# Query loads of the first two units in two-position packets, with two reorderings, in a retention kernel followed by a multiplicative FFN

## The chip, the cores and the metric

The kernel runs on one core of one Trainium2 chip. The metric is device time in microseconds of one execution, and lower is better. The time before is the median of three timed runs.

## What is computed

The reference computes retention attention with a decay per head, reshapes its output to one row per token, and feeds it to a feed-forward block whose two branches are multiplied.

```python
batch, n_heads, seq, head_dim = (8, 8, 576, 64)
n_tokens, d_model, d_ff = (4608, 512, 1024)

scores = scale * np.matmul(q, k.transpose(0, 1, 3, 2))
Dmat = np.where(rel >= 0, gamma[:, None, None] ** rel[None, :, :], 0.0)
attn = np.matmul(scores * Dmat[None, :, :, :], v)

x = attn.transpose(0, 2, 1, 3).reshape(B * S, H * D)
a = x @ w1
b = x @ w2
out = (a * b @ w3) @ w_out
```

Everything is float32. The weights reach the kernel as pairs of 32-bit words, eight bytes a value, and are turned into float32 on the chip.

## The kernel before, in words

**Units.** Two batch elements are treated together. The 576 positions are cut into five chunks, the first of 64 positions and four of 128. A pair of batch elements and a chunk make a unit `g`; there are 20 units, and unit 0 is the short chunk of the first pair.

**Attention of one unit.** `load` brings k, q and v of a unit into tiles `ld_k`, `ld_q`, `ld_v`, with a position on each partition and 64 floats of a head, 256 bytes, as one run. `scale` multiplies q and v by the decay of each position and head (`gq`, `gk`). `front` turns k and q with TensorE transposes into PSUM tiles `tp`, which ScalarE copies to `kT` and `qT`. `score` multiplies them (`sc`) and VectorE applies the causal mask (`pm`). `state` accumulates k times v over the chunks (`st`, copied by ScalarE to `sb`). `pv_state` and `pv` write the unit's output into `xps`, and ScalarE copies it to `xT`, the token matrix. Later units load q, and partly k, in blocks of 32 by 32 (`load_blocks`, tiles `bl_q`, `bl_k`) and turn them on VectorE (`front_blocks`); `scale_blocks` scales such q on GpSimd.

**Dense work.** `up` is one block of seven Strassen products of tokens with w1 and w2 (`up` tiles in PSUM, sums on VectorE in `plus`), and `down` is the same for the last product. While a dense block runs, `plus` takes one piece of other work from the list `aside` after each sum. In the first block, `up(..., first=True)`, one piece is taken before the first sum as well.

**Weights.** `conversion` turns each raw block (`raw`) into float32 in several steps on ScalarE and VectorE; `convert` runs a number of steps. The first dense block needs the four blocks "A" and the sums of `strassen_weights`.

**Order.** The order on each engine is the order of the program text, written out by hand. An instruction that waits holds back all that stand behind it on its engine. SyncE issues nearly all loads in that same order, and ScalarE issues that of the decays and of the first q. `keep_busy(n)` puts n matmuls of a 128 by 128 identity on TensorE; nothing reads their result.

The start of the program up to the first dense block is a straight list of calls. The part around the change reads, before:

```python
    load(1, "kq")
    ...
    scale(0, "q", engine=nc.vector)
    front(0, "k")
    keep_busy(4)
    front(0, "q")
    convert(2)
    score(0)
    scale(0, "v")
    state(0)
```

The decay of q arrives as `dq`, a head on each partition, and five TensorE transposes into `gps` with two VectorE copies give `gq`, a position on each partition.

Of the kernel before, what the change touches and what calls it, by code (L numbers as in the profile page):

```python
# [8 lines left out]
F32 = mybir.dt.float32  # L9
# [4 lines left out]
ALU = mybir.AluOpType  # L14
# [5 lines left out]
def kernel(  # L20
# [20 lines left out]
    P = 128  # L41
# [20 lines left out]
    const = ctx.enter_context(tc.tile_pool(name="const", bufs=1))  # L62
    wp = ctx.enter_context(tc.tile_pool(name="wp", bufs=1))
    ffn = ctx.enter_context(tc.tile_pool(name="ffn", bufs=2))
# [6 lines left out]
    pools = {}  # L71
# [13 lines left out]
    live = {}  # L85

    def load(g, names, engine=nc.sync):
        i, c = divmod(g, NC)
        sz = sizes[c]
        src = {"k": k, "q": q, "v": v}  # L90
        for nm in names:
            t = pools["ld"].tile([P, 2 * H, D], F32, tag="ld_" + nm, name="ld_" + nm)
            engine.dma_start(  # L93
                t[:sz], src[nm][2 * i:2 * i + 2, :, starts[c]:starts[c] + sz, :].rearrange("b h p d -> p (b h) d"))
            live[nm, g] = t

    dq = ffn.tile([P, 4, 2, TB], F32, tag="c", name="dq", bufs=1).rearrange("p a b s -> p (a b s)")[:H, :S]
    nc.scalar.dma_start(dq, decay_q)
    load(0, "k")
    load(0, "q", nc.scalar)  # L100

    ident = const.tile([P, P], F32, tag="ident", name="ident")
    make_identity(nc, ident)
# [16 lines left out]
    gps = acc.tile([P, NC, H], F32, tag="acc", name="gps")  # L120
    for c in range(NC):
        nc.tensor.transpose(gps[:sizes[c], c, :], dq[:, starts[c]:starts[c] + sizes[c]], ident[:H, :H])
    for c in (0, slice(1, NC)):
        n = short if c == 0 else P
        nc.vector.tensor_copy(gq[:n, c, :], gps[:n, c, :])

    def keep_busy(n):

        t = acc.tile([P, P], F32, tag="acc", name="idle")
        for _ in range(n):  # L130
            nc.tensor.matmul(t, ident, ident, start=True, stop=True)
# [53 lines left out]
    def front_blocks(g, names="kq"):  # L185
        c = g % NC
        n = sizes[c] // BL
        for nm in names:
            dst = pools["fr"].tile([P, 2, NP, P], F32, tag=nm + "T", name=nm + "T", bufs=1 if nm == "k" else 2)
            nc.vector.transpose(  # L190
                dst[:, :, :, :sizes[c]].rearrange("p b m (n x) -> p (b m) n x", x=BL),
                live["bl_" + nm, g][:, :, :n, :])
            live[nm + "T", g] = dst

    def scale(g, nm, scalar=False, engine=nc.gpsimd):
        c = g % NC
        sz = sizes[c]
        t, gam = live[nm, g], {"q": gq, "v": gk}[nm]
        t = t[:sz].rearrange("p (b h) d -> p b h d", b=2)
        if scalar:  # L200
            for h in range(H) if scalar is True else scalar:
                nc.scalar.mul(t[:, :, h, :], t[:, :, h, :], gam[:sz, c, h:h + 1])
            return
        engine.tensor_tensor(
            out=t, in0=t, in1=gam[:sz, c].unsqueeze(1).unsqueeze(3).to_broadcast([sz, 2, H, D]), op=ALU.mult)

    def front(g, names="kq"):
        c = g % NC
        sz = sizes[c]
        for nm in names:  # L210
            src = live[nm, g]
            dst = pools["fr"].tile([P, 2, NP, P], F32, tag=nm + "T", name=nm + "T",
                                   bufs=1 if nm == "k" and g >= NC else 2)
            for b in range(2):
                tp = acc.tile([P, NP, P], F32, tag="acc", name="tp")
                for p in range(NP):
                    h = b * H + 2 * p
                    nc.tensor.transpose(tp[:, p, :sz],  # L218
                                        src[:sz, h:h + 2, :].rearrange("p a d -> p (a d)"),
                                        ident[:sz, :sz])  # L220
                nc.scalar.copy(dst[:, b, :, :sz], tp[:, :, :sz])
            live[nm + "T", g] = dst

    def score(g):
# [100 lines left out]
    def load_block():  # L325
        n = loaded[0]
        if n == len(blocks):
            return
        key, w = blocks[n]
        t = raw.tile([P, CV, 2], I32, tag="raw", name="raw", bufs=5)  # L330
        if key[0] in ("A", "w12"):
            if key[0] == "A":
                _, r, f = key
                t4 = t.rearrange("p (j c n) t -> p j c n t", j=2, c=2)
                parts = [(t4[:, j], w[:, f * P:(f + 1) * P]) for j, w in enumerate((moe_w1, moe_w2))]
            else:
                _, fp, _, r = key
                parts = [(t.rearrange("p (c n) t -> p c n t", c=2), w[:, fp * QC:(fp + 1) * QC])]
            for t2, src in parts:
                src = src[2 * r * P:2 * (r + 1) * P]  # L340
                if r == 0:
                    nc.sync.dma_start(t2, src.rearrange("(c p) n t -> p c n t", p=P))  # L342
                else:
                    for half in range(2):
                        nc.sync.dma_start(t2[heads[half]],
                                          src.rearrange("(c a d) n t -> a d c n t", a=2, d=D)[1 - half])
        elif key[0] == "wo":
            src = w.rearrange("(a i x) n t -> i a x n t", i=KF, x=BL)[key[1]]
            for a in range(QP):
                nc.sync.dma_start(t[a * BL:(a + 1) * BL], src[a])  # L350
        else:
            _, ft, h = key
            src = w[ft * P:(ft + 1) * P].rearrange("(j r) (a h f) t -> h a r j f t", r=BL, a=QP, h=DF // CV)
            for a in range(QP):
                nc.sync.dma_start(t[a * BL:(a + 1) * BL].rearrange("p (j f) t -> p j f t", j=P // BL), src[h, a])
        live["raw", n] = t
        loaded[0] += 1
# [105 lines left out]
    def convert(n):  # L463

        for _ in range(n):
            if go_on() is not None:
                return
# [97 lines left out]
    aside, owed, spread, beside, loads = [], [], [], [], []  # L565
    g = 0
# [148 lines left out]
    load_block()  # L715
    load(0, "v")
    load_block()
    load(1, "kq")
    load_block()
    load(1, "v")  # L720
    load_block()
    scale(0, "q", engine=nc.vector)
    front(0, "k")
    keep_busy(4)
    front(0, "q")
    convert(2)
    score(0)
    scale(0, "v")
    state(0)
    convert_up_to(1)  # L730
# [27 lines left out]
    next(weight_sums)  # L758
    list(token_sums)
    list(weight_sums)  # L760
    aside.append(lambda: scale(2, "q", True))
    scale(2, "v")
    up(0, 0, 0, conv=[0, 0, 2, 2, 2], tail=False, first=True)
    front(2)
    convert(1)
    score(2)
    state(2)
# [364 lines left out]
    g = NC  # L1132
# [9 lines left out]
    for g in first_pair:  # L1142
        n = (1, 1, 2, 2)[g - NC]
        if not in_blocks[g + 2]:
            load(g + 2, "k")
            load_blocks(g + 2, "q")
        scale(g + 1, "v")
        if not in_blocks[g + 1]:
            front(g + 1, "k")
            front_blocks(g + 1, "q")  # L1150
        half = (n + 1) // 2
        if in_blocks[g + 1]:
            scale_blocks(g + 1)
            work(n - 1)
            aside.extend(lambda nm=nm: front_blocks(g + 1, nm) for nm in "kq")
            work(1)
            while aside:
                aside.pop(0)()
            half = 0
        if in_blocks[g + 2] and g + 2 < 2 * NC:  # L1160
            load_blocks(g + 2, "q")
            load_blocks(g + 2, "k")
        work(half)
        pv(g)()
        load(g + 2, "v", nc.scalar if in_blocks[g + 2] else nc.sync)
        if in_blocks[g + 2] and (g + 2) % NC != NC - 1:
            load(g + 2, "k")
        state(g + 1)
        score(g + 1)
        if not in_blocks[g + 2]:  # L1170
            scale_blocks(g + 2)
        if g == NC + 1:
            list(strassen_tokens(1, 0))
            forms = [(lambda h=h, second=second: spread.extend(weight_forms(h, second)),)
                     for h in halves for second in (False, True)]
            ups = [(up, 1, 0, fp) for fp in range(NQ)]
            todo.extend([*ups[:2], forms[0], *ups[2:], forms[2], (flush,), forms[1], (down, (1, 0), (1, 1)),
                         (down, (2, 2), (3, 2)), (open_second,), (down, (3, 0), (3, 1))])
        if not in_blocks[g + 1]:
            work(n // 2)  # L1180

    g = 2 * NC - 1
# [9 lines left out]
    g = 2 * NC  # L1192
# [15 lines left out]
    for g in range(2 * NC, G):  # L1208
        n = dealt[g - 2 * NC]
# [42 lines left out]
    g = G  # L1252
# [44 lines left out]
```

## Time and profile before

| | |
|---|---|
| median of 3 timed runs | 837.97 us (836.92 to 840.8) |
| profiled execution, its own time | 944.19 us |
| span of the profile | 942.5 us |
| mean granted TensorE clock in the profile | 0.846 |
| TensorE matmul busy | 931.7 us, 99% |
| VectorE, ScalarE, GpSimd busy | 545.4, 289.7, 224.4 us |
| bytes moved by DMA | 126.96 MB |

The profiled execution is longer than the timed runs; its clock is on record, that of the timed runs is not. A profile line gives start and duration in microseconds, then engine, source line, operation, the tile written and the tiles read, shapes and the number of instructions merged; what stands in brackets is the engine's idle time before it and what ended that. A float32 matmul stands in the trace as two records, so four identity matmuls are eight records. SPq and ACTq are the issuing sides of SyncE and ScalarE. In the first 30 us the queue that SyncE feeds moves 15,321 packets and 5.42 MB.

### The profile page before, as it was taken

The numbers are of one execution on the slowest core, as the hardware profiler recorded it, in microseconds if no ns is written. First come the engines' busy times: TensorE is split into PE (matmuls) and PEld (weight loads), VectorE is DVE, ScalarE is ACT, GpSimd is POOL, SyncE is SP. The second block draws the span as 40 slices with busy tenths as digits, with TensorE's granted clock in tenths as the row PEclk, the third lists the DMA queues.
The fourth block names the chain that finished last, engine by engine and source line by source line (L and its number), as shares of the span: only waits on it lengthen the run. The fifth ranks groups of instructions, "written<-read, shape, count | busy, mean of one in ns | idle before, by whom it ended". The sixth has DMA issues, their size and how long they took to land.

```text
span 942.5 us, 15780 instructions
## 1 busy us (share of the span) xinstructions
PE 931.7 (99%) x6101; PEld 818.4 (87%) x6101; DVE 545.4 (58%) x957; ACT 289.7 (31%) x601; POOL 224.4 (24%) x249
## 2 busy tenths in 40 slices
PE   8999999999999999899999999999999999999998
PEld 7999999533888998689999789998789998799976
DVE  4888888970544467644557643657545555535542
ACT  4776454560111111044343023331033320033200
POOL 1100010002003172015536015463016250044500
PEclk7888888888888888888888888888888888888888
DMA  9992543426045475967675146868245352135311
GB/s 187 225 222 74 83 122 98 133 62 99 1 86 111 74 224 197 319 173 194 170 193 154 41 88 207 215 192 160 57 116 192 119 184 73 40 131 187 118 29 40
DMA packets 197868, 126.96 MB, mean 135 GB/s; under 512 B 157848, under 2 KB 179608, under 8 KB 197792
## 3 DMA queue, kind: packets, MB, share of 16 engines
q1 hardware_dynamic: 167520, 50.14, 26.4%
q0 software_dynamic: 11632, 62.79, 20.4%
q10 hardware_dynamic: 18640, 13.02, 5.0%
q8 instruction: 48, 0.79, 0.4%
q14 instruction: 28, 0.23, 0.1%
HBM read 103.62 MB, written 22.28 MB: 134 GB/s over the span
## 4 chain that ended last, share of the span: by engine, by line
PE 95%; DMA 3%; SPq 1%; ACT 0%; POOL 0%; issue 0%; DVE 0%; ACTq 0%
PE po L637 26%; PE up L524 18%; PE up L1039 18%; PE seed L1039 13%; PE ps L477 7%; PE xps L299 4%; PE sc L233 4%; PE xps L274 2%; PE st L255 2%; PE tp L218 1%; DMA ld_v<-in_v_dram 1%; DMA kept<-wA 1%; DMA ld_q<-in_q_dram 1%; DMA out_dram<-ot 1%; SPq L93 0%; SPq L342 0%
## 5 line engine op out<-in xcount | busy, mean ns | idle before, releaser
L637 PE MATMUL po<-w3o,ab 128*128 128x256 f32 x552 | 145.0, 426 | 2.8 <-ACT ot L669 2.2
L637 PEld LDWEIGHTS po<-w3o,ab 128*128 128x128 f32 x552 | 109.4, 200 | 32.5 <-ACT ot L669 2.7
L1044 POOL TENSOR_TENSOR cc<-cc 128x384 f32<-128x384 f32 x112 | 109.3, 1002 | 5.2 <-ACT cc L1062 3.7
L1051 DVE TENSOR_TENSOR cc<-seed,cc 128x384 f32<-128x384 f32 x88 | 49.0, 557 | 91.9 <-PE seed L1039 85.4
L941 POOL DMA_DIRECT2D ra<-kept x53 | 30.0, 566 | 243.5 <-PE seed L1039 181.1
L1039 PE MATMUL up<-xT,ra 128*128 128x192 f32 x384 | 83.7, 360 | 0.0
L529 DVE TENSOR_TENSOR c<-up,c 128x384 f32<-128x384 f32 x80 | 44.0, 551 | 64.9 <-PE up L524 64.4
L524 PE MATMUL up<-xT,wA 128*128 128x192 f32 x384 | 80.5, 360 | 0.0
L637 PE MATMUL po<-wB,forms 128*128 128x256 f32 x288 | 75.8, 425 | 0.0
L524 PEld LDWEIGHTS up<-xT,wA 128*128 128x128 f32 x384 | 72.0, 197 | 1.4 <-issue 0.6
L1051 DVE TENSOR_TENSOR cc<-up,cc 128x384 f32<-128x384 f32 x88 | 48.5, 551 | 42.5 <-PE up L1039 39.8
L1039 PEld LDWEIGHTS up<-xT,ra 128*128 128x128 f32 x384 | 72.0, 198 | 1.3 <-issue 0.4
L637 PEld LDWEIGHTS po<-wB,forms 128*128 128x128 f32 x288 | 57.8, 201 | 15.2
L236 DVE TENSOR_TENSOR pm<-sc,mask 128x512 f32<-128x512 f32 (+1 forms) x80 | 45.4, 627 | 41.2 <-PE sc L233 41.1
L477 PE MATMUL ps<-wo,w3T 128*128 128x512 f32 x128 | 64.4, 673 | 0.0
L1058 ACT COPY seed<-up 128x384 f32<-128x384 f32 x56 | 25.9, 463 | 121.1 <-PE up L1039 118.5
L1039 PE MATMUL up<-ra 128*128 128x192 f32 x288 | 62.5, 359 | 0.0
L477 PEld LDWEIGHTS ps<-wo,w3T 128*128 128x128 f32 x128 | 25.5, 199 | 38.1 <-issue 37.8
L1039 PE MATMUL seed<-e,ra 128*128 128x192 f32 x256 | 57.4, 361 | 0.0
L1039 PEld LDWEIGHTS up<-ra 128*128 128x128 f32 x288 | 54.6, 198 | 0.2
L524 PE MATMUL up<-T,wS 128*128 128x192 f32 x256 | 53.5, 359 | 0.0
L181 POOL TENSOR_TENSOR bl_q<-bl_q,gqs 128x512 f32<-128x512 f32 (+1 forms) x26 | 27.9, 1093 | 103.3 <-DMA bl_q<-in_q_dram 101.3
(126 smaller groups left out, 1550.9 us busy)
## 6 DMA issues: line engine op xcount, KB each, us to landing
ra<-kept POOLq DMA_DIRECT2D x53, 896.0 KB, 4.9
raw<-in_moe_w_dram SPq DMA_DIRECT2D x72, 128.0 KB, 3.1
out_dram<-ot ACTq DMA_DIRECT2D x54, 128.0 KB, 2.3
bl_q<-in_q_dram SPq DMA_DIRECT2D x192, 32.0 KB, 3.0
bl_k<-in_k_dram SPq DMA_DIRECT2D x136, 32.0 KB, 3.0
raw<-in_moe_w_dram SPq DMA_DIRECT2D x16, 256.0 KB, 6.3
ld_k<-in_k_dram SPq DMA_DIRECT2D x8, 512.0 KB, 5.9
raw<-in_moe_w_out_dram SPq DMA_DIRECT2D x32, 128.0 KB, 2.7
```

The source lines that it names most:

```text
L181: nc.gpsimd.tensor_tensor(out=part, in0=part, in1=gqs[:, :, n0:n0 + n].unsqueeze(3).to_broadcast([P, NP, n, BL]), op=ALU.mult)
L233: nc.tensor.matmul(sc[j][:sz, p, :sz], kT[hs, b, p, :sz], qT[hs, b, p, :sz], start=True, stop=True)
L236: nc.vector.tensor_mul(pm[:sz, b, j, :, :sz], sc[j][:sz, :, :sz], mask[:sz, :sz].unsqueeze(1).to_broadcast([sz, NP, sz]))
L299: nc.tensor.matmul(banks[r][heads[half], b, n, :sz], vs[:sz, b * H + 2 * p + j, :], pm[:sz, b, j, p, :sz], start=(c == 0 and m == 0), stop ...
L477: nc.tensor.matmul(ps, live["w3T", ft][:, g, :], live["wo"][:, g, :], start=(g == 0), stop=(g == KF - 1))
L524: nc.tensor.matmul(ps[:, w, :], a[:, w, r, :], b[:, r, :], start=(new and w == r == 0), stop=(w == r == 1), skip_group_check=True)
L529: nc.vector.tensor_add(c[:, to], ps, c[:, sb])
L637: nc.tensor.matmul(ps[nm], a[A][:, f, :], live["W"][B][:, f, :], start=(f == 0 and not on), stop=(f == NP - 1), skip_group_check=True)
L941: engine.dma_start(ring[n % 3], kept[n % 14 // 7][nm])
L1039: nc.tensor.matmul(ps[:, w, :], weight_of(slot, a, w), B[b], start=(new and w == 0), stop=True, skip_group_check=True)
L1044: nc.gpsimd.tensor_tensor(out=o, in0=o, in1=i, op=ALU.add)
L1051: nc.vector.tensor_add(c[:, j], ps, with_add[:, j])
```

## The change

It has three parts.

1. **q of units 0 and 1.** `load_pairs` replaces `load` for these two. A partition then holds two neighbouring positions of one batch element, so that one run is 512 bytes, and a unit takes two DMAs, one for each batch element. The decay in this arrangement is `gq2`, made by `decay_pairs`: for each of the two positions a VectorE copy of `dq` into `by`, a TensorE transpose into `gps` and a VectorE copy out. `scale` becomes two VectorE instructions of half the size, which write to another tile, `q2`. `front` copies each PSUM tile of q with two ScalarE instructions that write every second element. `decay_pairs(1)` and `keep_busy(7)` stand where `keep_busy(4)` stood.
2. **The third unit.** The transposes of unit 2 are put on `aside` and so run between the products of the first dense block instead of after it, with two empty entries ahead of them.
3. **Blocks.** In the loop over `first_pair`, where both q and k of the next unit come in blocks (units 7, 8 and 9), VectorE turns those of q first, then, after an empty entry, those of k.

```diff
+    def load_pairs(g, engine):
+        i, c = divmod(g, NC)
+        sz = sizes[c] // 2
+        t = live["q", g] = pools["ld"].tile([P, 2 * H, D], F32, tag="ld_q", name="ld_q")
+        for b in range(2):
+            engine.dma_start(
+                t[b * sz:(b + 1) * sz].rearrange("p (h j) d -> p h (j d)", j=2),
+                q[2 * i + b, :, starts[c]:starts[c] + 2 * sz, :].rearrange("h (i j) d -> i h (j d)", j=2))
...
-    load(0, "q", nc.scalar)
+    load_pairs(0, nc.scalar)
...
+    def decay_pairs(c):
+        n = sizes[c] // 2
+        for j in range(2):
+            by = ffn.tile([H, 2, n], F32, tag="T", name="by", bufs=5)
+            nc.vector.tensor_copy(by, dq[:, starts[c]:starts[c] + 2 * n].rearrange(
+                "h (i j) -> h j i", j=2)[:, j].unsqueeze(1).to_broadcast([H, 2, n]))
+            nc.tensor.transpose(gps[:2 * n, 2 * c + j, :], by.rearrange("h b i -> h (b i)"), ident[:H, :H])
+            nc.vector.tensor_copy(gq2[:2 * n, c, j], gps[:2 * n, 2 * c + j, :])
+
+    decay_pairs(0)
...
+        if nm == "q" and g < 2:
...
+            for j in range(2):
+                engine.tensor_tensor(out=to[:sz, j * H:(j + 1) * H], in0=t[:sz].rearrange("p (h j) d -> p j h d", j=2)[:, j],
+                                     in1=gq2[:sz, c, j].unsqueeze(2).to_broadcast([sz, H, D]), op=ALU.mult)
+            return
...
-                nc.scalar.copy(dst[:, b, :, :sz], tp[:, :, :sz])
+                if nm == "q" and g < 2:
+                    for c2 in range(2):
+                        nc.scalar.copy(dst[:, c2, :, :sz].rearrange("p m (i j) -> p m i j", j=2)[:, :, :, b],
+                                       tp[:, :, c2 * sz // 2:(c2 + 1) * sz // 2])
+                else:
+                    nc.scalar.copy(dst[:, b, :, :sz], tp[:, :, :sz])
...
-    load(1, "kq")
+    load(1, "k")
+    load_pairs(1, nc.sync)
...
     front(0, "k")
-    keep_busy(4)
+    decay_pairs(1)
+    keep_busy(7)
     front(0, "q")
...
-    aside.append(lambda: scale(2, "q", True))
+    aside.extend([lambda: scale(2, "q", True), lambda: None, lambda: None,
+                  lambda: front(2, "k"), lambda: front(2, "q")])
     scale(2, "v")
     up(0, 0, 0, conv=[0, 0, 2, 2, 2], tail=False, first=True)
-    front(2)
...
-            aside.extend(lambda nm=nm: front_blocks(g + 1, nm) for nm in "kq")
+            aside.extend([lambda: front_blocks(g + 1, "q"), lambda: None, lambda: front_blocks(g + 1, "k")])
```

More of the change, by code (lines that the diff above doesn't have):

```diff
@@ L125 @@
         nc.vector.tensor_copy(gq[:n, c, :], gps[:n, c, :])
+    gq2 = const.tile([P, 2, 2, H], F32, tag="gq2", name="gq2")
+    def decay_pairs(c):
[7 more added lines that the diff above has]
+    decay_pairs(0)
     def keep_busy(n):
@@ L198, in scale @@
         t, gam = live[nm, g], {"q": gq, "v": gk}[nm]
+        if nm == "q" and g < 2:
+            if not g:
+                live["q2"] = ffn.tile([P, 2 * KF, TB], F32, tag="ab", name="q2").rearrange("p f t -> p (f t)")
+            n = 2 * H * D
+            to = live["q", g] = live["q2"][:, g * n:(g + 1) * n].rearrange("p (h d) -> p h d", d=D)
+            for j in range(2):
+                engine.tensor_tensor(out=to[:sz, j * H:(j + 1) * H], in0=t[:sz].rearrange("p (h j) d -> p j h d", j=2)[:, j],
+                                     in1=gq2[:sz, c, j].unsqueeze(2).to_broadcast([sz, H, D]), op=ALU.mult)
+            return
         t = t[:sz].rearrange("p (b h) d -> p b h d", b=2)
@@ L217, in front @@
                     h = b * H + 2 * p
[L218 to L221, printed above, removed]
+                    x = src[:sz, h:h + 2, :].rearrange("p a d -> p (a d)")
+                    nc.tensor.transpose(tp[:, p, :sz], x, ident[:sz, :sz])
+                if nm == "q" and g < 2:
[4 more added lines that the diff above has]
+                    nc.scalar.copy(dst[:, b, :, :sz], tp[:, :, :sz])
             live[nm + "T", g] = dst
```

## The prediction

> **What bounds the kernel now.** I read the page's busy times first, then the list of what TensorE waited for.
>
> ```profile
> PE 931.7 (99%) x6101; PEld 818.4 (87%) x6101; DVE 545.4 (58%) x957; ACT 289.7 (31%) x601; POOL 224.4 (24%) x249
> ```
>
> TensorE has work in 99% of the span, so only what shortens its idle or slow stretches can show. 4.2 of its 10.8 idle us lie before 60 us, and the largest later wait, 2.2 us at 397 us, is on a ScalarE copy behind output stores, which the change doesn't touch. So I read the start: the chain of waits, then TensorE in order of time, then stretches of 3.4 us.
>
> ```profile
> 1.45 6.23 DMA ld_q<-in_q_dram
> ...
> 9.62 2.81 SPq L93
> ...
> 15.37 7.96 DMA ld_v<-in_v_dram
> 23.33 0.07 issue
> 23.39 1.91 POOL ld_v L204
> 25.31 0.04 issue
> 25.35 1.21 PE st L255 x32
> ```
>
> The last to arrive ahead of the dense block at 29.58 us is v of unit 1, and its load was issued late behind the others.
>
> ```profile
> 6.94 1.25 PE L131 MATMUL idle<-ident 128*128 128x128 f32 x8
> 9.05 0.90 PE L218 MATMUL tp<-ident,ld_q 64*128 64x64 f32 x8 [0.86 <-DVE ld_q L204]
> 9.97 1.97 PE L233 MATMUL sc<-qT,kT 64*64 64x64 f32 x32
> 12.59 1.98 PE L255 MATMUL st<-ld_v,ld_k 64*64 64x64 f32 x32 [0.64 <-POOL ld_v L204]
> ...
> 20.33 1.18 PE L218 MATMUL tp<-ident,ld_q 128*128 128x128 f32 x8 [0.61 <-PE idle L131]
> 21.66 2.26 PE L233 MATMUL sc<-qT,kT 64*128 64x128 f32 x32 [0.16 <-ACT qT L221]
> 23.86 1.21 PE L274 MATMUL xps<-qT,sb 64*64 64x128 f32 x32
> 25.35 1.21 PE L255 MATMUL st<-ld_v,ld_k 128*64 128x64 f32 x32 [0.28 <-POOL ld_v L204]
> ```
>
> That v makes TensorE wait only 0.28 us: a second chain, q of unit 0 to q of unit 1, is nearly as late.
>
> ```profile
> 5.80:9.20 3.40, 2.54 (x25) 2.14 (x24) 1.68 (x4) 0.65 (x2) 0.00 (x0) 0.85 1.23 212
> 9.20:12.60 3.40, 2.73 (x42) 2.36 (x41) 2.19 (x6) 2.87 (x5) 1.89 (x1) 0.50 1.19 207
> 12.60:16.00 3.40, 3.40 (x64) 3.40 (x64) 2.54 (x5) 1.36 (x3) 0.00 (x0) 0.50 1.36 222
> 16.00:19.40 3.40, 3.40 (x21) 3.28 (x18) 1.78 (x3) 2.85 (x6) 0.00 (x0) 0.50 1.18 272
> ```
>
> Third from the right is the granted clock: half from 9.2 to 19.4 us; then DMA share and GB/s. DMA is full throughout.
>
> **What the Trainium skill says.** "TensorE: Matmul & The Clock Gate", Part 1, says the clock halves after an idle window of about 3.4 us and returns after a busy one, and that windows run free of the kernel. The trace agrees: half clock lasts 10.2 us, three windows. The same page, Part 4, says transposes don't count as busy for the gate; here the window with 1.25 us of identity matmuls and short transposes lost the clock. "DMA: Bandwidth & Descriptors", Specifications, puts the smallest run at full rate at 512 bytes. The packet records of this trace have medians of 18 ns for 256 bytes, 27 for 512 and 46 for 1,024, so two 256-byte packets cost 36 and one of 512 costs 27.
>
> **Part 1, gain.** q of unit 0 is 1,024 packets of 256 bytes, 64 on each of 16 engines: 64 x 18 = 1.15 us become 32 x 27 = 0.86, 0.3 us less. Unit 1 is twice that, 0.6 us less. With v behind both, v of unit 1 can land about 0.9 us sooner (0 if packets are cut again, 1.6 if a packet's cost is the same at both sizes). Each unit issues one DMA more: on ScalarE's queue that is 0.74 us ahead of the decay `gk` and the table load (3.58 us to 4.3; the first copy is at 6.79, so it is hidden; `gk` still lands ahead of v, which it scales). On SyncE it is about 0.6 us ahead of a raw block and v of unit 1, and lies inside the time in which that queue is held back (the 2.81 us above).
>
> **Part 1, cost.** One pass of `decay_pairs` is copy, transpose, copy: 0.16 (row `gq<-gps`) + 0.05 (VectorE's end at 8.99 to TensorE's start at 9.04) + 0.24 (0.20 for such a transpose, and part of its weight load) + 0.04 + 0.16 = 0.65 us, and two follow each other: 1.3 us. In the changed program's order `decay_pairs(0)` stands after the two `gq` copies (end 6.66) and before k's transposes, so k's move from 6.29 to about 7.8; hidden, since q's scaling ends later. q's scaling starts at 7.96 in place of 7.77, two halves of 0.63, end 9.2. **The decisive step**: the transposes of `decay_pairs(1)` wait for VectorE copies that stand behind q's scaling, and `keep_busy(7)` and q's transposes stand behind them on TensorE. Until now the filler ran while q was awaited; now it starts when q is ready: 9.2 + 1.1 = 10.3. Seven matmuls are 14 records of 0.156 us at the granted 0.85 (1.25/8), 2.2 us, or of 0.22 at half clock (1.76/8), 3.1 us. So q's transposes start at 12.5 to 13.4, not at 9.05.
>
> The four ScalarE copies: a copy of 256 elements takes 0.37 us, one of 512 0.59, so 128 elements cost about 0.27; I assume no penalty for writing every second element (bounds 0 and twice). `score(0)` needs the third copy and starts at 13.6 to 14.8 (9.97 before). The delay doesn't pass on in full: `state(0)` had its own wait for v (12.59), and takes 1.2 at best, 2.0 at half clock, so it ends at 16.1 to 18.8, not 14.57. Behind it stand ScalarE's `sb` copy (0.58), three steps of the second raw block (2.25), two VectorE steps (1.4), then half of q's scaling of unit 1 (0.65; before it was 1.22 whole): 21.0 to 23.7. Transposes and three copies later `score(1)` starts at 22.8 to 25.9, against 21.66. Less the 0.28 that v no longer costs, the dense block starts 0.9 to 3.9 us later. The sooner landing of v is then off the path. The four extra transposes beyond this, and VectorE's 1.3 us for eight small copies, are in these sums.
>
> **Part 2.** The same 16 transposes and four copies move; nothing is added. `score(2)` waits 0.18 us for ScalarE's copy now; between products the copy is hidden. ScalarE's `c` copy comes about 2.3 us later and delays the product `ab` by 0.5 us on VectorE; `pm` follows at 44.3 and is needed at 48.08. Gain 0.2 us, bounds 0 to 0.5. Cover gone: nothing worse than now.
>
> **Part 3.** VectorE turns q at 296.4, 318.9 and 346.4, where it turned k. GpSimd ended their scaling at 290.8, 312.8 and 339.8. k of unit 8 is turned some 3 us later, done by 323.2, against `score` at 329.9; of unit 9 by 350.7, against 356.6. In these stretches TensorE has no wait. The sum pushed behind them (L613, 0.69 us) is read at about 366.9. On SyncE, blocks of q for units 8 and 9 can be issued 1.5 us sooner and those of k 1.5 us later, in the order in which the buffers are asked for. Zero; bounds -0.3 and +0.3.
>
> **Sum.** +0.9 to +3.9, less 0.2; I take +1.9, nearer the lower end because some windows may be granted full clock. Against the profile: 944.19 + 1.9. That execution is 12.7% above the median at a granted 0.846; the difference is in long products that the change leaves alone, and the start hangs on DMA, ScalarE and VectorE too, so I carry the same microseconds to 837.97: **839.9 us**.
>
> **Rivals.** *(a) Seven fillers win the clock back*: if the window holding them counts as busy, score, state and transposes run at 1.2 instead of 2.0 us. The delay is the lower end: 837.97 + 0.9 - 0.2 = 838.7. For: the fillers are what ended the half clock at 19.4. Against: they fill 2.3 of the 3.4 us to 12.6. *(b) Slower*: the half clock lasts longer, because the window in which unit 1's k and filler now fall is broken by the wait for its q. Eight transposes take 1.97 at half clock and 1.18 after, so each more window costs 3.4 x (1 - 1.18/1.97) = 1.4 us. With two, +1.9 + 2.7 = 842.6. It decides from about 26 us: if TensorE is at 0.5 there. *(c) Transfers bound the start after all*: v of unit 1 lands 0.9 to 1.6 sooner, the half clock is gone as well (9.6 us of work, up to 3.9 saved, partly waited away), about -4.3: 833.7. Against: the queue order above. *(d) Packets of 512 bytes don't come about*: then only costs remain, but the gain is off the path already: 839.9.
>
> **How the numbers follow.** Forecast with (d) 0.47, (a) 0.22, (b) 0.23, (c) 0.08. A measurement of this kernel can tell about 0.5% (4.2 us) from no change. Faster is (c), 0.08; slower is most of (b) and the forecast's upper tail, 0.25; the rest, 0.67, is within. The range 835.0 to 844.0 leaves out half of (c) and the worst of (b); the forecast's own is 838.5 to 841.7.
>
> **What would show it.** In the changed profile: filler after q's scaling and not before; `score(0)` at 13.6 to 14.8; `score(1)` at 22.8 to 25.9; v of unit 1 landing before 23 us with no wait of `state(1)` on it; dense start at 30.5 to 33.5; no `score(2)` wait; no TensorE wait between 290 and 360 us. It is wrong if q's transposes start before 11 us, or if the dense block starts before 29.6.

## The result, and the profile after

The changed kernel took 843.87 us (median of 10 runs, 841.43 to 849.7), the kernel before beside it 839.17 us (10 runs, 836.92 to 840.8). The ratio is **1.0069, interval [1.0044, 1.0094]**: 4.7 us between the medians, slower by more than the 0.5% that a measurement can tell. The forecast was 839.9 us and no change. The measured 843.87 us lies just inside the stated range of 835.0 to 844.0 us, but that is the range's width and not the reckoning: that one had +1.9 us where +4.7 came, and the kernel before itself took 1.2 us more beside it than the 837.97 us from which it started.

The profiled execution of before ran at a granted clock of 0.846; times below are therefore compared with another profile of the same kernel, called the copy of before (clock 0.992, own time 841.25 us). The profile after took 848.36 us itself, near the upper end of its runs, so the lengths in it show mechanisms; sizes come from medians.

The page's line of busy times for the changed kernel:

```profile
PE 823.7 (97%) x6111; PEld 742.6 (88%) x6111; DVE 548.0 (65%) x967; ACT 289.9 (34%) x605; POOL 224.8 (27%) x249
```

TensorE still has work nearly always, so the loss must again lie in its idle or half-speed stretches. The chain of waits of the changed kernel runs through the start like this (start and length in us, engine, tile, line):

```profile
1.83 6.13 DMA ld_q<-in_q_dram
...
8.08 1.28 DVE q L227 x2
...
10.21 0.27 PE gps L144
10.48 3.29 PE idle L153 x14
13.76 0.63 PE tp L250 x4
...
15.17 1.86 PE sc L268 x29
...
21.71 0.70 DVE e L448
...
23.05 2.40 DVE q L227
...
27.38 2.13 PE sc L268 x16
...
32.75 2.07 issue
...
37.88 0.48 DVE xT L531
...
38.50 1.54 PE up L559 x8
```

The chain now goes from q of unit 0 (8.08) over the decays into the filler, which is on the path with its full 3.29 us, and on to `score(0)` at 15.17. From there it runs over the weight conversions to q of unit 1 (23.05), to `score(1)` (27.38) and to the token sum `xT`, for which the dense block's second product waits until 38.50. In the chain of before that the prediction shows, the filler of unit 0 did not appear and v of unit 1 was the last to arrive; in that of the copy of before it doesn't appear either.

TensorE in order of time, first the copy of before, then the changed kernel (in brackets the idle time ahead and what ended it):

```profile
9.86 1.15 PE L233 MATMUL sc<-qT,kT 64*64 64x64 f32 x32 [0.21 <-ACT qT L221]
21.18 2.06 PE L233 MATMUL sc<-qT,kT 64*128 64x128 f32 x32 [0.24 <-ACT qT L221]
28.75 4.07 PE L524 MATMUL up<-xT,wA 128*128 128x192 f32 x24
...
42.42 2.47 PE L233 MATMUL sc<-qT,kT 64*128 64x128 f32 x32 [2.65 <-ACT qT L221]
```

```profile
25.58 1.33 PE L250 MATMUL tp<-ident,q 128*128 128x128 f32 x8 [1.84 <-DVE q L227]
27.38 3.28 PE L268 MATMUL sc<-qT,kT 64*128 64x128 f32 x32 [0.47 <-ACT qT L253]
...
38.50 2.84 PE L559 MATMUL up<-xT,wA 128*128 128x192 f32 x16 [1.58 <-DVE xT L531]
...
48.22 2.06 PE L268 MATMUL sc<-qT,kT 64*128 64x128 f32 x32
```

`score(0)` moved from 9.86 to 15.17, `score(1)` from 21.18 to 27.38, where the same 32 records take 3.28 instead of 2.06 us; the first dense product starts at 35.45 instead of 28.75. `score(2)` no longer waits for ScalarE. The 2.65 us in the copy of before are its own, though: other profiles with the old order have 0.18 to 0.45 us there. The stretches of 3.4 us of the changed kernel (granted clock third from the right):

```profile
12.60:16.00 3.40, 3.04 (x30) 2.63 (x31) 0.73 (x1) 1.55 (x6) 0.18 (x1) 0.50 1.25 209
22.80:26.20 3.40, 1.56 (x12) 1.22 (x10) 3.40 (x4) 0.38 (x1) 2.09 (x1) 0.95 1.05 217
26.20:29.60 3.40, 2.93 (x25) 2.59 (x26) 0.97 (x3) 3.27 (x7) 0.00 (x0) 0.55 1.31 220
```

The seven fillers did not win the clock back in this execution. It came at 23 us, TensorE was busy for only 1.56 us of the next stretch because it waited for q of unit 1, and at 26.6 us the clock was halved a second time, under `score(1)`.

In the six other profiles of kernels with the same seven fillers at the same place the clock did come back behind them. In that of part 1 alone, `score(0)` shows it (1.08 instead of 1.86 us for the same 29 records):

```profile
15.03 1.08 PE L268 MATMUL sc<-qT,kT 64*64 64x64 f32 x29 [0.45 <-ACT qT L253]
```

In the traces the clock changes only at steps of 3.41 us, and these windows lie differently in each execution. Here the window that began at 9.50 us, ahead of the filler, held 2.97 us of TensorE work; in the other six the window began at 9.66 to 10.8 us and held 3.13 to 3.42 us. The same program thus has more than one course of the start.

One more row decides: VectorE and GpSimd beside each other in order of time, the changed kernel first:

```profile
22.66 2.23 POOL L235 TENSOR_TENSOR ld_v<-ld_v,gk 128x1024 f32<-128x1024 f32 x1 [9.88 <-DMA ld_v<-in_v_dram]
...
23.05 2.99 DVE L227 TENSOR_TENSOR q<-ld_q,gq 128x512 f32<-128x512 f32 x2
...
31.88 2.46 POOL L235 TENSOR_TENSOR ld_v<-ld_v,gk 128x1024 f32<-128x1024 f32 x1 [7.00 <-DMA ld_v<-in_v_dram]
...
32.61 2.27 DVE L461 SCALAR_TENSOR_TENSOR wA<-m,e 128x512 f32<-128x512 f32 x1
```

Then the copy of before:

```profile
22.37 2.48 DVE L236 TENSOR_TENSOR pm<-sc,mask 128x512 f32<-128x512 f32 x4 [1.12 <-PE sc L233]
...
22.96 1.90 POOL L204 TENSOR_TENSOR ld_v<-ld_v,gk 128x1024 f32<-128x1024 f32 x1 [10.54 <-DMA ld_v<-in_v_dram]
...
32.17 1.97 POOL L204 TENSOR_TENSOR ld_v<-ld_v,gk 128x1024 f32<-128x1024 f32 x1 [7.30 <-DMA ld_v<-in_v_dram]
...
32.29 2.39 DVE L149 TENSOR_TENSOR wS<-wA,wS 128x512 f32<-128x512 f32 x1
```

GpSimd scales v of units 1 and 2 when their loads land, near 22.7 and 32 us in both kernels. In the copy of before, the first scaling fell under `pm`, which reads PSUM and was not slowed, and the second met a `wS` sum that nothing on the path waited for. In the changed kernel VectorE is later, and the same two scalings meet the scaling of q of unit 1 (2.99 us; without such a meeting 1.28) and `wA` (2.27 instead of 0.69). Both are on the chain; the 2.07 us of "issue" at 32.75 are that second meeting. The Trainium skill, "SBUF — State Buffer", section "Who interferes with whom", states that a VectorE instruction with two inputs in SBUF contends with a GpSimd instruction that reads SBUF, and that one with at most one such input, outside the two-port modes, doesn't; `pm` and the two slow instructions agree, and the price here is 1.6 to 1.7 us a meeting.

Which instruction is met differs from one execution to the next. Parts 1 and 2 without part 3 are the same program up to 290 us; in their profile q of unit 1 was through before the scaling of v could slow it, and the conversion step behind it was met instead (2.13 us, elsewhere 0.42):

```profile
21.06 1.29 DVE L227 TENSOR_TENSOR q<-ld_q,gq 128x512 f32<-128x512 f32 x2
21.76 2.35 POOL L235 TENSOR_TENSOR ld_v<-ld_v,gk 128x1024 f32<-128x1024 f32 x1 [9.15 <-DMA ld_v<-in_v_dram]
22.26 2.13 DVE L434 TENSOR_SCALAR m<-raw 128x512 int32<-128x512 int32 x1
```

### The profile page after: what moved, and what is told of

Same layout as the page of the kernel before. It is cut to its first block, busy times and chain, and to the rows that moved or that the text cites. A ratio compares the mean times of both kernels' runs of the same rounds, so it can differ in the third digit from the quotient of the medians.

```text
span 846.6 us, 15825 instructions
## 1 busy us (share of the span) xinstructions
PE 823.7 (97%) x6111; PEld 742.6 (88%) x6111; DVE 548.0 (65%) x967; ACT 289.9 (34%) x605; POOL 224.8 (27%) x249
## 2 busy tenths in 40 slices
DMA packets 196364, 126.96 MB, mean 150 GB/s; under 512 B 154808, under 2 KB 178104, under 8 KB 196288
## 4 chain that ended last, share of the span: by engine, by line
PE 87%; DVE 5%; DMA 4%; issue 2%; ACT 1%; SPq 0%; POOL 0%; ACTq 0%; DVEq 0%; POOLq 0%
PE po L672 23%; PE up L1076 17%; PE up L559 15%; PE seed L1076 13%; PE ps L512 6%; PE sc L268 4%; PE xps L334 4%; PE xps L309 2%; PE st L290 2%; DMA out_dram<-ot 1%; PE tp L250 1%; DMA ra<-kept 1%; DMA ld_q<-in_q_dram 1%; DVE e L448 1%; DVE pm L271 1%
## 5 line engine op out<-in xcount | busy, mean ns | idle before, releaser
L672 PE MATMUL po<-w3o,ab 128*128 128x256 f32 x552 | 126.2, 383 | 3.9 <-ACT ot L704 2.3
L1076 PE MATMUL up<-xT,ra 128*128 128x192 f32 x384 | 74.3, 330 | 2.3 <-DMA ra<-kept 2.3
L559 PE MATMUL up<-xT,wA 128*128 128x192 f32 x384 | 70.7, 328 | 1.6 <-DVE xT L531 1.6
L1076 PEld LDWEIGHTS up<-xT,ra 128*128 128x128 f32 x384 | 64.2, 191 | 3.6 <-DMA ra<-kept 2.6
L559 PEld LDWEIGHTS up<-xT,wA 128*128 128x128 f32 x384 | 63.3, 190 | 3.0 <-issue 2.3
L672 PE MATMUL po<-wB,forms 128*128 128x256 f32 x288 | 65.9, 382 | 0.0
L1095 ACT COPY seed<-up 128x384 f32<-128x384 f32 x56 | 25.9, 463 | 102.5 <-PE up L1076 63.3
L512 PE MATMUL ps<-wo,w3T 128*128 128x512 f32 x128 | 55.1, 592 | 0.0
L1076 PE MATMUL up<-ra 128*128 128x192 f32 x288 | 54.8, 326 | 0.0
L1076 PE MATMUL seed<-e,ra 128*128 128x192 f32 x256 | 50.9, 329 | 0.0
L559 PE MATMUL up<-T,wS 128*128 128x192 f32 x256 | 46.7, 326 | 1.4 <-DVE wS L171 1.4
```

What stands on the lines that cost most here:

```text
L512: nc.tensor.matmul(ps, live["w3T", ft][:, g, :], live["wo"][:, g, :], start=(g == 0), stop=(g == KF - 1))
L559: nc.tensor.matmul(ps[:, w, :], a[:, w, r, :], b[:, r, :], start=(new and w == r == 0), stop=(w == r == 1), skip_group_check=True)
L672: nc.tensor.matmul(ps[nm], a[A][:, f, :], live["W"][B][:, f, :], start=(f == 0 and not on), stop=(f == NP - 1), skip_group_check=True)
L1076: nc.tensor.matmul(ps[:, w, :], weight_of(slot, a, w), B[b], start=(new and w == 0), stop=True, skip_group_check=True)
```

## The experiments

Starts read from one profile each, in us, and what the runs gave:

| kernel | score(0) | score(1), its length | first product, wait of the second | score(4) | ratio [interval] |
|---|---|---|---|---|---|
| copy of before | 9.86 | 21.18, 2.06 | 28.75, 0 | 69.73 | |
| changed | 15.17 | 27.38, 3.28 | 35.45, 1.58 | 75.70 | 1.0069 [1.0044, 1.0094] |
| part 1 alone | 15.03 | 26.06, 3.78 | 35.34, 0.87 | 73.62 | 1.0061 [1.004, 1.0082] |
| part 2 alone | 10.76 | 21.84, 2.06 | 28.92, 0 | 68.51 | 1.0005 [0.9988, 1.0023] |
| part 3 alone | 10.73 | 22.69, 2.06 | 29.53, 0.30 | 67.80 | 0.9987 [0.9977, 0.9998] |
| parts 2, 3 | 11.14 | 22.82, 2.06 | 29.66, 0.30 | 69.16 | 0.9994 [0.9977, 1.0012] |
| parts 1, 2 | 14.71 | 23.60, 3.58 | 32.03, 1.52 | 72.22 | 1.0047 [1.0026, 1.0067] |
| parts 1, 2, no filler | 11.71 | 22.12, 2.06 | 28.96, 0.31 | 67.95 | 1.0001 [0.9984, 1.0018] |
| changed, no filler | 11.81 | 22.21, 2.06 | 29.30, 0 | 68.02 | 1.0005 [0.9976, 1.0035] |
| changed, filler and decays elsewhere | 12.98 | 23.39, 2.06 | 30.23, 0.32 | 69.22 | 0.9997 [0.9977, 1.0016] |
| parts 1, 2, four fillers | 14.11 | 24.74, 2.06 | 31.59, 2.02 | 72.27 | 1.0037 [1.0024, 1.0049] |
| before, 7 fillers behind q | 13.53 | 24.03, 2.06 | 30.87, 0.30 | 69.14 | 1.0004 [0.9986, 1.0022] |
| before, 21 fillers behind q | 17.89 | 29.05, 3.31 | 37.15, 0.65 | 75.22 | 1.0102 [1.0075, 1.0129] |
| changed, one gate | 14.45 | 23.33, 3.66 | 31.78, 1.71 | 72.15 | 1.0086 [1.0056, 1.0117] |
| parts 1, 2, long filler | 14.68 | 23.57, 2.06 | 30.41, 0.30 | 69.94 | 1.0101 [1.0072, 1.013] |
| parts 1, 2, long filler, two gates | 14.56 | 23.45, 2.06 | 30.30, 0.29 | 69.26 | 1.0068 [1.0041, 1.0095] |
| before, long filler | 9.86 | 22.62, 2.06 | 29.47, 0.30 | 67.85 | 1.0023 [1.001, 1.0036] |
| changed, two gates | 15.02 | 23.91, 3.34 | 32.34, 0 | 70.77 | 1.0034 [1.0017, 1.0052] |

Profiles of the same program up to 290 us differ at `score(4)` by 1.9 us (copy of before, part 3 alone) and by 3.5 us (changed; parts 1, 2), so that column is good to no better than 3.5 us.

**The parts.** The first run is the copy of before, for its profile; then each part by itself.

> The kernel before, for a profile to set beside that of the changed kernel. Start-chain theory (the filler and the unit-1 decays stand behind q's scaling on TensorE, and the shift lets GpSimd's scaling of v meet VectorE operations that read two SBUF tiles): dense block of the first tokens begins at 29 to 30.5 us and runs its first 24 matmul records without a wait; VectorE's scaling of q takes 1.22 us in both units, and no weight step (L399 to L426) takes over 0.8 us before 30 us. Rival (the loss is made later, in the dense blocks): the first dense block begins within 1.5 us of the changed kernel's 35.5 us.

The first dense product came at 28.75 us and its 24 records ran without a wait, as the start-chain theory had it. Part 1 alone is the changed kernel with parts 2 and 3 put back:

```diff
-    aside.extend([lambda: scale(2, "q", True), ..., lambda: front(2, "q")])
+    aside.append(lambda: scale(2, "q", True))
...
+    front(2)
...
+            aside.extend(lambda nm=nm: front_blocks(g + 1, nm) for nm in "kq")
```

> Before plus part 1 alone (q of units 0 and 1 in pairs, decays, filler of seven). Start-chain theory: it carries the whole loss, 4.5 to 7 us over before. Rival, parts 2 and 3 carry it: within 2 us of before.

Part 2 alone and part 3 alone are the diff's other two pieces put into the kernel before.

> Before plus part 2 alone (transposes of the third unit inside the first dense block). Start-chain theory: -0.8 to +0.5 us, as the prediction had it. Rival (ScalarE's copies inside the block push back the conversion steps, which the second block waits for): 2 to 4 us slower.

> Before plus part 3 alone (blocks of k turned behind those of q). Start-chain theory: -0.5 to +0.5 us. Rival (VectorE gives k later than the score of the unit needs it, or loads of k blocks come late): 1 to 3 us slower.

Part 1 alone loses 5.1 us, as much as the whole. Part 2 alone gives nothing that shows at the end; in its profile `score(2)` still waited 1.66 us for ScalarE. Part 3 alone is faster by 0.13%, the only kernel here whose interval lies below 1; with 17 intervals, one that ends at 0.9998 can be chance. Without part 3 the other two lose 3.9 us:

> The changed kernel without part 3 (k's blocks turned first, as before). Start-chain theory: part 1 carries the loss, so 843 to 845.5 us. Block theory (part 3 makes the score of unit 9 wait for k's blocks in some runs, up to 3.7 us and a half-clock window, once the loads of its blocks land late): the median falls by 0 to 1.5 us, and the runs above 847 us are gone.

The forecast that no run would lie above 847 us missed: three of 22 took 847.6 to 848.9 us. Six executions of parts 1 and 2 and twelve of before had the same mean granted clock, 0.994, and took 843.4 and 839.4 us on average: 4.0 us are lost at equal clock, so less granted clock over the whole run is not the main cost.

Parts 2 and 3 together:

> The kernel before with parts 2 and 3, without part 1: the two parts that cost nothing alone (0.9987 and 1.0005). Expected 0.998 to 1.000: the start of before, no wait of score(2), first dense product at 28 to 29 us. If parts 2 and 3 harm each other (k's blocks of unit 9 late, as in three of the kernels that have part 3): 1.001 to 1.003, and a wait of a score near 321 us in the profile.

837.99 against 839.62 us; the interval holds 1, so it isn't shown to beat before. What the change loses is part 1.

**Which piece of part 1.** The filler taken out, from the changed kernel and from parts 1 and 2:

```diff
     decay_pairs(1)
-    keep_busy(7)
     front(0, "q")
```

> The changed kernel without the seven filler matmuls. Queue theory (the filler stands on the path to unit 0's score): q's transposes of unit 0 start at 10.4 to 10.6 instead of 13.7 us, and the median is 2 to 3.5 us under the changed kernel (840.5 to 842). Clock rival (the filler pays by winning the clock back): the half clock lasts longer, score and state of units 0 and 1 take 2 us each, and the time is within 1 us of the changed kernel or above it.

> Parts 1 and 2 without the seven fillers and without part 3. Queue theory with the block theory: 836.5 to 839.5 us, and no run above 845, where the same kernel with part 3 had 845.8, 847.9 and 850.4. Rival (those late runs come from part 1's changed start): they stay.

The whole loss is gone in both, with pairs, decays, half-size copies and all. (Three of the 14 runs with part 3 took 845.8 to 850.4 us, none without it more than 843.2.) The other way round, the filler kept in its old place and length, ahead of the wait, and the decays of unit 1 put behind q's transposes:

```diff
-    decay_pairs(1)
-    keep_busy(7)
+    keep_busy(4)
     front(0, "q")
+    decay_pairs(1)
```

> The changed kernel with four filler matmuls ahead of q's wait as before, and the decays of unit 1 made behind q's transposes. Queue theory: q's transposes start at 9.0 to 9.6 us, GpSimd's scaling of v meets VectorE's mask products again, q's scaling of unit 1 takes 1.3 us, and nearly the whole loss is gone: 838.5 to 841 us. Collision rival alone (the filler is not what counts): 842 or more.

Gone as well, though q's transposes began at 10.85 us, later than expected. Then four fillers in the new place:

```diff
-    keep_busy(7)
+    keep_busy(4)
```

> Parts 1 and 2 with the four identity matmuls of the kernel before, at the new place behind decay_pairs(1), in place of seven. q's transposes about 0.7 us (at full clock) to 1.3 us (at half clock) sooner than with seven. If the seven win the clock back too early, four may leave it at half until 20 us, and score(1) at full clock as without filler: first dense product at about 30 us, ratio 1.000 to 1.002. If only the delay counts: first dense product at about 31, ratio 1.003.

3.1 us are lost even so, and in this profile `score(1)` ran at full clock (2.06 us): a halved clock there is not needed for a loss. The line that holds it, in its TensorE timeline:

```profile
35.07 2.84 PE L559 MATMUL up<-xT,wA 128*128 128x192 f32 x16 [2.02 <-DVE xT L531]
```

The token sum ended last, at 2.26 us instead of 0.55, because GpSimd's scaling of v of unit 2 met it. In this profile VectorE reached the mask products `pm` at 25.94 us and did not wait for `score(1)`; in that of parts 1 and 2 it reached them at 25.50 us and waited 0.80 us in all for the products of `score(1)` at half clock. Both were through with `pm` at 28.4 to 28.5 us.

**The delay alone.** The kernel before, with fillers that can only start when q of unit 0 is scaled:

```diff
-    keep_busy(4)
+    late = acc.tile([P, P], F32, tag="acc", name="idle")
+    nc.tensor.matmul(late, ident[:short, :], live["q", 0][:short, 0:2, :].rearrange("p a d -> p (a d)"), ...)
+    keep_busy(6)
     front(0, "q")
```

> The kernel before with its four fillers replaced by seven, the first of which reads the scaled q of unit 0, so that all stand behind q's scaling; q comes in single positions and no decays are made. Queue theory: q's transposes start at 11 to 12.2 us, and the filler alone costs 3 to 6 us over before, through the later score, the later weight steps and meetings of VectorE with GpSimd. Rival (the pairs and their decays are what costs): within 1.5 us of before.

A miss: nothing was lost. `score(0)` is 3.7 us later, the first product 2.1, `score(4)` within the spread of before. With 20 in place of 6:

> The kernel before, with 21 identity matmuls between k's and q's transposes of unit 0 in place of four, the first of which reads scaled q. No pairs, no decays, no other order: a late start and nothing else. Seven such matmuls put the first dense product at 30.87 us, and cost nothing at the end; 14 more at 0.22 to 0.3 us put it at 34 to 35, about where the changed kernel (35.45) and part 1 alone (35.34) have it. Slack theory (the first 2 to 3 us of delay fall into later waits, above all the 2.65 us of score(2), the rest passes on): 5 to 6 us late, 2 to 4 us lost, ratio 1.0025 to 1.005. Theory that the delay alone is harmless and that only the half clock at score(1) and VectorE's meetings with GpSimd cost: within 0.1% of before. If it costs as much as part 1 alone (1.006), the start time is all that counts and there is no slack.

8.6 us lost, more than expected, with no pairs and no decays in the kernel. Its start has the changed kernel's marks: `score(1)` at half clock (3.31 us), a wait of the second product, `score(4)` at 75.22. So filler that starts late is enough, and what it costs is not proportional. In the table every kernel whose `score(0)` starts at 14.11 us or later loses at least 2.9 us, and none up to 13.53 loses anything that shows, but for the long filler in the kernel before, treated below. The first dense product doesn't sort them so: two of the kernels with the long filler have it at 30.3 to 30.4 us, sooner than the 30.87 of a kernel that loses nothing. Whether some of the 8.6 us is a cost of 21 matmuls as such, and not of the delay, was not separated.

**The meetings with GpSimd.** A one-column GpSimd copy of the scaled q ahead of the scaling of v of unit 1 holds that scaling back until VectorE is through with q:

```diff
     convert(2)
+    gate = const.tile([P, 2], F32, tag="gate", name="gate")
+    nc.gpsimd.tensor_copy(gate[:, 0:1], live["q", 1][:, 2 * H - 1, D - 1:D])
     scale(1, "v")
```

> The changed kernel with one GpSimd copy of a column of unit 1's scaled q ahead of the scaling of unit 1's v, so that GpSimd begins after VectorE has ended. Collision theory (an operation of VectorE that reads two SBUF tiles waits for the whole GpSimd operation that it meets): q's scaling of unit 1 takes 1.3 us instead of 2.99, score(1) begins 1.5 to 1.8 us sooner, and the median is 1 to 2 us under the changed kernel. Rival (VectorE was slow for its 256-element rows with gaps, not for GpSimd): it still takes about 3 us, and the time is the same.

q took 1.29 instead of 2.99 us, as it also does without a gate in the profile of parts 1 and 2, so this alone doesn't show what the gate did. The held scaling met the next conversion (2.41 instead of 0.69), v of unit 2 met the token sum (2.25 instead of 0.55), and the second product waited 1.71 us. 7.2 us were lost. A later row of this profile adds to that:

```profile
326.37 3.15 PE L268 MATMUL sc<-qT,kT 64*128 64x128 f32 x32 [3.72 <-DVE kT L212]
```

k of unit 9 was turned late: VectorE stood idle for 8.56 us ahead of it until its blocks had landed, one of them 10.6 us after it was issued. Such a wait of `score` is seen only in kernels with part 3, in which the blocks of q come first. A second gate holds v of unit 2 behind the last weight sum:

```diff
+    nc.gpsimd.tensor_copy(gate[:, 1:2], A(0, "S4")[:, 1, 1, P - 1:P])
     scale(2, "v")
```

> As the last one, and a second such copy, of the last weight sum, ahead of the scaling of unit 2's v. Collision theory: the weight step at L461 takes 0.7 us instead of 2.3, the first dense block loses its wait for VectorE's token sum (1.6 us), and the median is 2 to 3.3 us under the changed kernel. Rival: no further gain over the single gate.

With both, the wait of the second product is gone, `score(4)` starts at 70.77 instead of 72.22 to 75.70, and 2.9 us are lost instead of 4.7 to 5.8 (0.69% of 839.17); the intervals overlap, so the gain is likely rather than shown. The second gate alone, without filler, where no such meeting was on the path:

> The same with one GpSimd copy of the last weight sum ahead of the scaling of unit 2's v, so that it no longer meets VectorE's weight sums at 33 us. Collision theory: that weight sum takes 0.7 us instead of 2.4, the second dense block's wait of 1.4 us at 55 us is shorter, and the median is 0.5 to 2 us under the ungated one. Rival (VectorE has slack there): no difference.

1.0000, interval [0.9983, 1.0017]: the gate itself costs nothing that shows. The wait of 1.41 us that it was to shorten is 1.41 us in both profiles.

**The half clock.** Parts 1 and 2, with the filler ahead of q of unit 1 long enough to cover TensorE's wait for it:

```diff
     front(1, "k")
-    keep_busy(4)
+    keep_busy(12)
```

> Parts 1 and 2 with 12 identity matmuls in place of four ahead of q's transposes of unit 1: they fill the 2.25 us for which TensorE waited there. Clock theory: score(1) at full clock, 2.06 us instead of 3.58, q's transposes at the same time, so the first dense product at about 30.5 instead of 32.0 us; parts 1 and 2 gave 1.0047, this gives 1.002 to 1.003. Collision theory (VectorE's sums, slowed by GpSimd's scaling, end last): the 1.5 us come back as a longer wait of the dense block's second product, 3.0 instead of 1.52 us, and the ratio stays at 1.004 to 1.005.

> Parts 1 and 2 with the 12 identity matmuls ahead of q's transposes of unit 1, and with GpSimd's scalings of v of units 1 and 2 held until VectorE's scaling of q of unit 1 and the last weight sum are done. Takes away both suspected costs: score(1) at full clock and no meeting of VectorE and GpSimd ahead of the dense block. Both theories: first dense product at about 31 us, no wait of the second one, ratio 0.999 to 1.001. If it stays above 1.003, the cost of part 1 is neither of the two, nor the start.

(The second has both gates too.) The start did what the clock theory said: `score(1)` at 2.06 us, first product at 30.41 and 30.30, waits of 0.30 and 0.29, `score(4)` at 69.94 and 69.26. The end did not: 1.0101 [1.0072, 1.013] and 1.0068 [1.0041, 1.0095]. Both theories of the start missed here. By what was written down before the last of these runs, a ratio above 1.003 means that the cost of part 1 is neither the half clock, nor the meetings, nor the start; with 1.0068 this holds, except for what the longer filler itself costs. In the first profile the time is lost late:

```profile
560.61 1.65 PE L1076 MATMUL up<-xT,ra 128*128 128x192 f32 x4 [3.22 <-DMA ra<-kept]
```

Saved sums read back from memory came 3.22 us late, and the half clock followed (the four records take 1.65 instead of 0.92 us). In the copy of before that wait is 0.37 us. The same filler in the kernel before:

> The kernel before with 12 identity matmuls in place of four ahead of q's transposes of unit 1, and nothing else. Parts 1 and 2 with this longer filler lost 8.5 us, though their profile stood at 121 us where that of before stands; this asks whether the longer filler itself costs something later. Slack theory: the first dense product at 30 to 31.5 us, as with seven fillers at the earlier place, ratio 0.999 to 1.001. If the longer filler has a cost of its own: 1.003 or more. If what was lost came by chance of a few runs, or from part 1: as the slack theory.

1.0023, interval [1.001, 1.0036], between the two forecasts, with `score(4)` at 67.85: the longer filler costs 1.9 us that its start doesn't show. Why it does, and why 8 us were lost beside part 1, stays open; one profile each is too little to tie the late waits to it.

## Why the prediction was wrong

**Right.** The decisive step was the one named: the filler now starts when q is ready (10.41; forecast 10.3). Taking it out or moving it back takes the loss away. Packets fell from 197,868 to 196,364, so runs of 512 bytes did come about, and no gain from them shows: q of unit 0 landed at 7.96 us, against 7.68 in the profile before, and though GpSimd took up v of unit 1 at 22.66 instead of 23.39 us, `state(1)` did not wait for it, as forecast. (The bound of 1.6 us for equal packet costs is 1.7 by its own figures, 96 packets of 18 ns; nothing hangs on it.) The copies that write every second element cost no more than assumed: four took 0.87 us for unit 0 and 1.36 for unit 1. Part 2's wait of `score(2)` is gone from the changed profile, and the gain of 0.2 us is below what runs show (1.0005).

**Wrong: three terms of part 1's cost, each outside its range.**

- *The filler and q's transposes.* The fillers took 3.36 us for 14 records, past the 3.1 of half clock, and q's transposes began at 13.69 instead of 12.5 to 13.4; `score(0)` came at 15.17 instead of 13.6 to 14.8. A small miss, 0.4 us beyond the upper end.
- *From `score(0)` to `score(1)`.* The conversions were sized right (three ScalarE steps 2.26 us against 2.25, two VectorE steps 1.4). "Half of q's scaling of unit 1 (0.65)" was not: it met GpSimd and the first half was ready only 2.4 us after its start. `score(1)` at 27.38 instead of at most 25.9. The step asked what VectorE has to do, and not who else works at that moment.
- *From `score(1)` to the dense block.* The forecast moved this stretch unchanged, 7.6 us to the first product; it took 8.1, so the first product's 35.45 us, instead of 30.5 to 33.5, is mostly made by the steps before. What the forecast put at nothing is the wait of the second product, 1.58 us: `wA` took 1.6 us longer beside GpSimd's scaling of v of unit 2, and at half clock `score(1)` gave VectorE its first products 2.1 us after its start, in the copy of before 1.2.

The sum +1.9 thus stands against +4.7 to +5.8 measured. Of these terms only the wait of the second product fails in every profile of a kernel with part 1 unaltered (1.58 us, 1.52 with parts 1 and 2, 0.87 with part 1 alone): in that of parts 1 and 2, `score(1)` at 23.60 and the first product at 32.03 lie inside the forecast, and 3.9 us are lost all the same, where the forecast had 3.7 at most and 1.9 as its figure. How the rest of the loss comes about is not shown. The argument "the difference is in long products that the change leaves alone" was harmless: the copy of before puts the first product at 28.75, 0.8 us from the profile used.

**Rival (b)**, given 0.23, is what the profile shows by its own sign: clock 0.55 from 26.2 to 29.6, after a wait of 1.84 us for q of unit 1. At the start the clock was at half for 13.65 and 3.41 us, two windows more than the 10.24 us of the profile before, and the rival's +4.6 us is close to the +4.7 between the medians. But half-clock time doesn't sort the kernels: seven fillers in the kernel before had 13.65 us of it and lost nothing, parts 1 and 2 had 6.83 and lost 3.9, and with four fillers there was none at `score(1)` and 3.1 us were lost. What these share is a late VectorE, with GpSimd's scalings, whose time the loads set, meeting work on the path. That this makes the loss is argued and not shown: with both gates the gain was likely only, and with both gates and the long filler 5.7 us were lost.

**Rival (a)** came true as to the clock and not as to the time. In six of the seven profiles with these fillers the clock was back at 13.1 to 14.2 us; but TensorE ran ahead, waited 2.24 to 2.26 us for the same q of unit 1 in the four without the long filler, and was at half clock again at `score(1)`.

**Part 3's zero** held for the time (faster by 0.13% alone), not for the claim of no wait between 290 and 360 us: k of unit 9 came late by 3.72 us with one gate, by 1.29 us with filler and decays elsewhere and by 0.69 us without filler; kernels without part 3 show no such wait. The step that failed is "blocks of k 1.5 us later", taken as harmless. The changed kernel's own profile has waits of 1.17 and 0.52 us in that stretch, for output sums and not for k.

**Open.** Which of the later waits (output stores at 360 us, saved sums at 560 us) are caused by a late start and which merely vary: the changed kernel's own profile has 2.28 and 2.31 us there, the copy of before 4.04 and 0.37. These waits are as large as what is to be explained. TensorE in the changed kernel stands 6.0 us behind the copy of before at `score(4)`, 3.1 at 377 us, still 3.1 at 544 us, and 6.7 from 587 us to the end. The last step is made here, by the wait and a window of half clock behind it (1.62 instead of 0.92 us):

```profile
562.40 1.62 PE L1076 MATMUL up<-xT,ra 128*128 128x192 f32 x4 [2.31 <-DMA ra<-kept]
```

This wait is 1.85 to 3.22 us in six profiles, all of kernels that lose, and at most 1.48 in the others, four of which lose too. No run took it away, so the start's part in the loss and this one's are not told apart.

## What to carry to other kernels

Filler that keeps the clock up is free only while it stands ahead of a wait; an instruction put before it that itself needs the awaited data turns all of it into delay on the path. When a chain is delayed, look at what the other engines do at the new times, above all GpSimd beside VectorE: here a `score(0)` 3.7 us late cost nothing that shows, and one 4.3 us late or more cost 2.9 to 8.6 us. A part whose profile is harmless at the start can still lose at the end, so the runs decide, not the marks.

## What the hardware showed that was not expected

- A 0.69 us VectorE instruction with two SBUF inputs takes 2.27 us when it meets a GpSimd multiplication of 128x1024; the int32 scalar operation on `raw` (0.42 us) took up to 2.13. Four `pm` products with an input in PSUM took 2.48 us beside the same scaling and 2.49 without it. The one that began first kept its time: in the profile of parts 1 and 2 the second half of q, begun just ahead of GpSimd, still took 0.69 us, and GpSimd took 2.35 instead of 1.90.
- A wait of TensorE of 1.84 to 2.26 us, shorter than a window of 3.41 us, was followed by half clock in the changed kernel and in four of the experiments, so no window without work was needed. Windows with 0.63 to 1.75 us of TensorE work were followed by half clock (part 1 alone from 21.05 us, two gates from 21.02), windows with 1.83 us (changed kernel from 36.81) and 1.90 us (four fillers from 33.56) were not. Busy time alone doesn't decide: in the profile before, a window with 2.56 us (from 5.78) was followed by half clock too.
